# Two cached-attention decodes on one core: q in bank pairs, four products in a row, single heads at the end

## The chip, the cores and the metric

The kernel runs on 1 core of one Trainium2 chip. The metric is the device time of one execution in microseconds (us); the median of several runs is compared. The kernel before takes 674.53 us (median of 3 runs, 673.84 to 674.82).

## The reference

Two independent attention blocks, A and B, each decode one token. All tensors are bf16.

```python
def _A_ref(x, k_cache, v_cache, wq, wo):        # x [1,1,512], caches [1,32,8192,128]
    q = (x @ wq).reshape(B, Sq, 32, 128).transpose(0, 2, 1, 3)
    scores = einsum("bhqd,bhkd->bhqk", q, k_cache) * (128 ** -0.5)
    p = softmax(scores, axis=-1)
    o = einsum("bhqk,bhkd->bhqd", p, v_cache)
    return o.transpose(0, 2, 1, 3).reshape(B, Sq, 4096) @ wo      # wo [4096, 512]
# _B_ref is the same with B's inputs (32 query heads, 32 key heads)
return concatenate([a, b], axis=-1)
```

For each block 32 heads read a K cache and a V cache of 2 MiB a head, and `wq` and `wo` are 4 MiB each. Together that is 272 MiB, 285.2 MB, read once; the arithmetic on it is small.

## The kernel before

The caches are worked through in 16 **quads** of 4 heads (`NM` = 16: quads 0 to 7 of A, 8 to 15 of B). A quad's K is 8 MiB, laid out as 128 partitions of 64 KiB: partition 32h + p holds 256 consecutive keys of head h. Its V has the same layout. `kn` holds two quads of K, `vn` one quad of V. At the start `vn` holds both `wq`; at the end `kn` holds both `wo`.

**Loads.** SyncE (SP) issues every load, in one fixed order, with semaphore waits in between (lines 190 to 210): wq of A, x of A and B, wq of B, K0, K1, V0, K2, V1, then K(n+1) and V(n) in turn, then wo. V0 waits until q has left `vn` (`s_q`), K2 until TensorE has read quad 0's products out of `kn` (`s_red`), V(n) until the matmuls with V(n-1) are done (`s_pv`), and K(n+1) until the first product of quad n (`s_mul`). A load later in the order is not issued before an earlier one, whatever it needs itself. After the last K come all of wo of A, wo of B's first 16 heads, the last V in two pieces (cut at key `VCUT` of each partition's 256), and wo of B's other heads in the pieces of the table `WOB`. `WP` names pieces that are loaded in two parts, partitions 0 to 119 and 120 to 127.

**q.** TensorE begins in the block `pe_first`. x is broadcast into `xb`, then x @ wq is formed in four groups (A and B, two each) of 16 matmuls: 4 PSUM banks of `big`, 4 matmuls a bank (line 353). ScalarE (ACT) copies the 4 banks to `qbc` in bf16 (line 376), 32 partitions of each, and only then TensorE starts the next group (line 358).

**A quad.** VectorE (DVE) multiplies K in place by q, broadcast over the keys, in four products of 64 keys (`mul`, line 427). TensorE sums each product over the 128 dims down to 8 partial sums, with 16 matmuls against the identity that add up in one PSUM bank (a *chunk*, lines 256 and 259). DVE adds these 8 (`sr`, line 432) to get scores. A chunk uses bank c % 2 of `big`, so chunk 2 waits for `sr(0)` and chunk 3 for `sr(1)`. DVE's order is `mul(0) mul(1) mul(2) sr(0) mul(3) sr(1) sr(2) sr(3)`; then it takes the maximum, and ACT does four exponentials into `pt`.

**V.** TensorE's loop (line 247) does quad n's four chunks first and then quad n-1's V matmuls: the sums of the exponentials (line 298), 64 matmuls of `pt` with `vn` (line 309), and, after ACT's copy of the result (line 382), 8 small matmuls that lay the heads out as columns (line 315). The last round has no chunks: it multiplies wo of A and of B's first 16 heads instead (line 281), then does the V matmuls of quad 15. In these, before the second piece of V, it issues 8 matmuls with a zero vector (line 304) and then waits for that piece (`s_v1`).

**The end.** Heads 16 to 31 of B go through `oz`, whose columns are the stationary operands of `rows(g)` (line 231), 4 matmuls a head. Heads 28 and 29 get there by way of `zb`, one matmul and a copy (lines 491, 323 and 494), heads 30 and 31 by a copy (line 492). DVE copies the result (line 496), and SP and ACT store it (line 502).

Of the kernel before, what the change touches and what calls it, by code (L numbers as in the profile page):

```python
# [6 lines left out]
ALU = mybir.AluOpType  # L7
# [7 lines left out]
def bass_concat_heads__mha_block_cached__gqa_block_cached__decode_kernel(  # L15
# [14 lines left out]
    ks = [A_k_cache, B_k_cache]  # L30
# [3 lines left out]
    NA = 2  # L34
# [4 lines left out]
    C = D // P  # L39
# [19 lines left out]

    WOB = [(0, 16), (16, 8), (24, 4), (28, 2), (30, 1), (31, 1)]  # L60
    HT = 16
    RG = [32, 16, 8, 4, 2]
    WP = {2: 120}
    VCUT = T - CT
    NQ = NOUT // P
    QR = P // NQ

    with ExitStack() as st:
# [5 lines left out]
        def flat(ap):  # L74
            return ap.rearrange("p t d -> p (t d)")
# [4 lines left out]
        assert T * Dh == NA * W  # L80
        wq_v = flat(vn[:]).rearrange("p (a c j i h d) -> p a c j i h d", a=NA, c=C, j=2, i=4, h=G)
        KX = 1
# [112 lines left out]
        load_k(1, (s_xm, 2))  # L195
        load_v(0, (s_q, 4 * NA * 2))
        load_k(2, (s_red, RED), (s_k, 32))
# [18 lines left out]
        e = nc.tensor  # L216
        rw, rq = [e.alloc_register("pe_" + x) for x in ("rw", "rq")]
        n1, k1, rv, ko = [e.alloc_register("pe_" + x) for x in ("n1", "k1", "rv", "ko")]
        nc.br("pe_first", engines=[nc.tensor.engine])
        with nc.body("pe_main", valid_engines=[nc.tensor.engine]):  # L220
# [16 lines left out]
            e.reg_mov(k1, 1)  # L237
            e.reg_mov(rv, 0)
            e.reg_mov(ko, 0)
            e.wait_ge(c_pool, POOL)  # L240

# [5 lines left out]
            with e.Fori(0, NM + 1) as n:  # L247
                nr = e.alloc_register("pe_nr")
                e.reg_sub(nr, n1, 1)
                with e.If_lt(nr, NM):  # L250
                    with e.Fori(0, NCH) as c:
                        e.wait_ge(s_mul, k1)
                        e.wait_ge(s_sr, k1)
                        e.reg_add(k1, k1, 1)
                        o = big[:, bass.ds(c % 2, 1), :].rearrange("p o (t d) -> p (o t) d", d=DW)
                        e.matmul(o, ident[:], chunk(0), start=True, stop=False, skip_group_check=True)  # L256
                        with e.Fori(0, RL):
                            for u in range(RU):
                                i = e.matmul(o, ident[:], chunk((1 + u) * DW), start=False,  # L259
                                             stop=(u == RU - 1), skip_group_check=True)  # L260
# [35 lines left out]
                with e.If_ne(nr, 0):  # L296
                    e.wait_ge(s_p, n1)
                    e.matmul(misc[:, 0:G], ones_f[:], rsum[:], start=True, stop=True).then_inc(s_sum, 1)  # L298
                    e.wait_ge(s_v, rv)
                    for j in range(T // NT):  # L300
                        if j * NT == VCUT:
                            with e.If_eq(nr, NM):
                                for _ in range(8):
                                    e.matmul(big[0:1, 0, :], zero[:], wo_sb[:, 0, :], start=True,
                                             stop=True)
                                e.wait_ge(s_v1, 16)
# [11 lines left out]
                e.reg_add(n1, n1, 1)  # L318
                e.reg_add(rv, rv, 16)
# [12 lines left out]
        with nc.body("pe_first", valid_engines=[nc.tensor.engine]):  # L332
            for r, v in ((rw, 1), (rq, G)):
                e.reg_mov(r, v)
            e.sem_inc(s_sum, 1)
            e.sem_inc(s_turn, 1)
            e.sem_inc(s_w[1], 1)
            e.wait_ge(s_x, 16 * NA)
            e.wait_ge(c_on, 1)
            for a in range(NA):  # L340
# [6 lines left out]
            with e.Fori(0, NA) as a:  # L347
                e.wait_ge(s_w[1], rw)
                e.reg_add(rw, rw, 16)
                with e.Fori(0, 2) as j:  # L350
                    with e.Fori(0, G) as hh:
                        for c in range(C):
                            i = e.matmul(  # L353
                                big[:, bass.ds(hh, 1), :].rearrange("p o (i d) -> p (o i) d", d=Dh),
                                xb[:, a, c, :], wq_v[:, a, c, j, :, hh, :],
                                start=(c == 0), stop=(c == C - 1))
# [8 lines left out]
        rq, n1 = [e.alloc_register("act_" + x) for x in ("rq", "n1")]  # L365
        e.reg_mov(rq, G)
        e.reg_mov(n1, 1)
        e.sem_inc(s_p, 1)
        for a in range(NA):
            e.wait_ge(s_xm, a + 1)  # L370
            e.copy(xb[:, a].rearrange("p c m -> p (c m)"), (misc, tps)[a]).then_inc(s_xb, 1)  # L371
        with e.Fori(0, NA * 2) as j:
            e.wait_ge(s_q, rq)
            for hh in range(G):
                q = slice(hh * HP, (hh + 1) * HP)
                e.copy(qbc[q, bass.ds(j * 4, 4), :].rearrange("p i d -> p (i d)"),  # L376
                       big[q, hh, :]).then_inc(s_qc, 1)
            e.reg_add(rq, rq, G)
        e.wait_ge(c_pool, POOL)
# [24 lines left out]
        s_o = sem("s_o")  # L404
        for r, v in ((n1, 1), (k5, RL), (rk, 16), (kt, 0), (ks, NCH + 2)):
            e.reg_mov(r, v)
        e.sem_inc(s_sr, 2)
        e.sem_inc(s_k, 16)
# [8 lines left out]
        i.then_inc(c_sel, 1)  # L417
        e.wait_ge(s_qc, 2 * G)
        e.wait_ge(s_k0, 16)
        with e.Fori(0, NM):  # L420
# [9 lines left out]
            def sr(c):  # L430
                e.wait_ge(s_red, k5)
                e.tensor_reduce(s_sb[:, c * CT:(c + 1) * CT],  # L432
                                big[:, c % 2, :].rearrange("p (t d) -> p t d", d=DW),
                                AX.X, ALU.add).then_inc(s_sr, 1)
# [98 lines left out]
```

## Time and profile before

| what | value |
|---|---|
| median of 3 runs | 674.53 us |
| the profiled execution, its own time | 674.37 us |
| its span, first to last instruction | 673.1 us |
| busy: PE, DVE, ACT | 405.5, 337.0, 80.9 us |
| moved by DMA | 285.24 MB, mean 424 GB/s |
| DMA engines busy, share of the span | 98.5% |

The profile divides the span into 40 slices of 16.8 us; a row gives each slice's DMA rate. Windows give the same for any stretch: a DMA packet counts where it starts, with all its bytes, so in a short window a packet of 64 KiB can be counted by itself. The PE clock in the profile is the share of full speed that TensorE was granted. "Released by" names what ended a wait; "issue" is time in which the profile shows nothing waited for. Times below are from the span's start unless a duration is meant.

### The profile page before, as it was taken

How to read it: one execution, taken by the hardware profiler on the slowest of the kernel's cores; microseconds unless marked ns; L12 is line 12 of the kernel's file. 1: busy time of each engine (PE TensorE's matmuls, PEld its weight loads, DVE VectorE, ACT ScalarE, POOL GpSimd, SP SyncE). 2: the span in 40 equal slices, each digit the busy share in tenths (PEclk: the TensorE clock that was granted, in tenths of full speed). 3: DMA queues.
4: the chain of work that ended last, by engine and by line, in shares of the span. 5: the costliest groups of instructions: out<-in, count | busy, mean ns of one | idle time of the engine just before them, and what ended most of it. 6: DMA issues, size and time to landing. Idle time of an engine off the chain costs nothing.

```text
span 673.1 us, 8068 instructions
## 1 busy us (share of the span) xinstructions
PE 405.5 (60%) x2415; PEld 168.2 (25%) x2415; DVE 337.0 (50%) x218; ACT 80.9 (12%) x182; POOL 2.4 (0%) x13
## 2 busy tenths in 40 slices
PE   1667595919376481927558192855729194663986
PEld 0222232303122130313223031322313031221333
DVE  1036676638092654719174471908356280926510
ACT  1211202020202002020200202020110202020020
POOL 1000000000000000000000000000000000000000
PEclk9767897969779596977869596886959687795987
DMA  9999987999999999999999999999999999999898
GB/s 373 438 436 436 432 378 312 436 436 436 436 436 436 436 436 432 421 417 425 425 436 436 436 436 436 436 436 436 436 436 436 436 436 436 436 436 436 387 439 297
DMA packets 6071, 285.24 MB, mean 424 GB/s; under 512 B 690, under 2 KB 949, under 8 KB 1205
## 3 DMA queue, kind: packets, MB, share of 16 engines
q1 hardware_dynamic: 6063, 285.22, 98.5%
q8 instruction: 1, 0.02, 0.0%
q14 instruction: 1, 0.01, 0.0%
q10 hardware_dynamic: 6, 0.00, 0.0%
HBM read 285.21 MB, written 0.00 MB: 424 GB/s over the span
## 4 chain that ended last, share of the span: by engine, by line
DMA 72%; DVE 11%; PE 10%; issue 4%; ACT 1%; SPq 1%; DVEq 0%; ACTq 0%
DMA kn<-in_B_k_cache_dram 40%; DMA kn<-in_A_k_cache_dram 25%; DVE kn L427 10%; PE big L259 5%; DMA kn<-in_B_wo_dram 4%; PE big L353 4%; DMA kn<-in_B_x_dram 2%; ACT qbc L376 1%; PE acc L309 1%; DVE s_sb L432 1%; SPq L173 1%; PE big L256 0%; DVEq L422 0%; PE tps L315 0%; ACT acc_sb L371 0%
## 5 line engine op out<-in xcount | busy, mean ns | idle before, releaser
L427 DVE TENSOR_TENSOR kn<-kn,qbc x64 | 280.1, 4419 | 155.6 <-DMA kn<-in_B_k_cache_dram 70.7
L259 PE MATMUL big<-kn,ident 128*128 x960 | 266.3, 419 | 0.0
L256 PE MATMUL big<-kn,ident 128*128 x64 | 28.1, 440 | 216.5 <-DVE kn L427 196.4
L259 PEld LDWEIGHTS big<-kn,ident 128*128 128x128 bf16 x960 | 100.8, 105 | 149.7 <-issue 99.4
L432 DVE TENSOR_REDUCE s_sb<-big 128x64 f32<-128x512 f32 x64 | 42.7, 686 | 73.4 <-PE big L259 73.4
L382 ACT COPY acc_sb<-acc 128x512 f32<-128x512 f32 x16 | 9.4, 585 | 474.9 <-PE acc L309 474.8
L256 PEld LDWEIGHTS big<-kn,ident 128*128 128x128 bf16 x64 | 6.3, 98 | 234.8 <-issue 232.9
L309 PE MATMUL acc<-vn,pt 128*16 128x512 bf16 x1024 | 60.5, 387 | 2.4 <-DMA vn<-in_B_v_cache_dram 2.4
L388 ACT ACTIVATE pt<-s_sb,negb 32x256 bf16<-32x256 f32 x64 | 54.8, 857 | 1.3
L452 DVE TENSOR_TENSOR oD<-tps,rinv 128x4 f32 x16 | 2.6, 162 | 75.8 <-PE tps L315 75.7
L353 PE MATMUL big<-vn,acc_sb 128*128 x64 | 25.2, 579 | 12.9 <-issue 12.9
L309 PEld LDWEIGHTS acc<-vn,pt 128*16 128x16 bf16 x1024 | 24.7, 91 | 29.9 <-DMA vn<-in_B_v_cache_dram 2.5
L315 PE MATMUL tps<-tsel,acc_sb 128*128 128x4 f32 x128 | 16.9, 255 | 11.1 <-ACT acc_sb L382 10.4
L315 PEld LDWEIGHTS tps<-tsel,acc_sb 128*128 128x128 f32 x128 | 15.5, 191 | 19.1 <-ACT acc_sb L382 17.9
L353 PEld LDWEIGHTS big<-vn,acc_sb 128*128 x64 | 8.7, 135 | 29.3 <-issue 28.0
L388 ACT ACTIVATION_READ_ACCUMULATOR pt<-s_sb,negb 32x1 f32 x64 | 15.9, 248 | 0.0
L376 ACT CAST qbc<-big 32x512 f32 x16 | 9.2, 576 | 30.8 <-PE big L353 30.5
L281 PE MATMUL big<-kn,o 128*1 x48 | 12.2, 418 | 0.0
L298 PE MATMUL misc<-rsum,ones_f 128*128 128x4 f32 x32 | 6.0, 259 | 6.9 <-issue 6.2
L384 ACT ACTIVATE negb<-gm 128x1 f32<-128x1 f32 x16 | 3.2, 203 | 46.3 <-DVE gm L455 46.3
L342 PE MATMUL misc<-ones_bf,kn 1*128 1x128 bf16 x4 | 0.6, 302 | 13.2 <-DMA kn<-in_B_x_dram 13.2
L298 PEld LDWEIGHTS misc<-rsum,ones_f 128*128 128x128 f32 x32 | 4.8, 188 | 13.8 <-issue 13.8
(50 smaller groups left out, 40.9 us busy)
## 6 DMA issues: line engine op xcount, KB each, us to landing
vn<-in_B_v_cache_dram SPq DMA_DIRECT2D x1, 6144.0 KB, 20.5
vn<-in_A_wq_dram SPq DMA_DIRECT2D x1, 4096.0 KB, 13.7
vn<-in_B_wq_dram SPq DMA_DIRECT2D x1, 4096.0 KB, 22.3
kn<-in_A_wo_dram SPq DMA_DIRECT2D x1, 4096.0 KB, 24.3
kn<-in_B_wo_dram SPq DMA_DIRECT2D x1, 2048.0 KB, 28.9
vn<-in_B_v_cache_dram SPq DMA_DIRECT2D x1, 2048.0 KB, 25.1
kn<-in_B_wo_dram SPq DMA_DIRECT2D x1, 1024.0 KB, 27.4
kn<-in_B_wo_dram SPq DMA_DIRECT2D x1, 480.0 KB
```

Of the source, the lines that this page charges most:

```text
L256: e.matmul(o, ident[:], chunk(0), start=True, stop=False, skip_group_check=True)
L259: i = e.matmul(o, ident[:], chunk((1 + u) * DW), start=False, stop=(u == RU - 1), skip_group_check=True)
L281: i = e.matmul(y, o2[:, bass.ds(h + u, 1)], wo_sb[:, h + u, :], start=False, stop=False, skip_group_check=True)
L298: e.matmul(misc[:, 0:G], ones_f[:], rsum[:], start=True, stop=True).then_inc(s_sum, 1)
L309: i = e.matmul(acc[q:q + NT * G, :], pt[:, ts, :].rearrange("p t g -> p (t g)"), vn[:, ts, :].rearrange("p t d -> p (t d)"), start=(j < NP ...
L315: i = e.matmul(tps[:, 0:G], acc_sb[:, t * Dh:(t + 1) * Dh], tsel[:, t * G:(t + 1) * G], start=(t == 0), stop=(t == NT - 1))
L353: i = e.matmul(big[:, bass.ds(hh, 1), :].rearrange("p o (i d) -> p (o i) d", d=Dh), xb[:, a, c, :], wq_v[:, a, c, j, :, hh, :], start=(c = ...
L376: e.copy(qbc[q, bass.ds(j * 4, 4), :].rearrange("p i d -> p (i d)"), big[q, hh, :]).then_inc(s_qc, 1)
L382: e.copy(acc_sb[:], acc).then_inc(s_acc, 1)
L388: i = e.activation(pt[q, :, h], s_sb[q, :], AF.Exp, bias=negb[q, :], scale=scale, accum_out=rsum[q, h:h + 1])
L427: e.tensor_tensor(k, k, qbc[:, bass.ds(n, 1), :].broadcast_to([P, CT, Dh]), ALU.mult).then_inc(s_mul, 1)
L432: e.tensor_reduce(s_sb[:, c * CT:(c + 1) * CT], big[:, c % 2, :].rearrange("p (t d) -> p t d", d=DW), AX.X, ALU.add).then_inc(s_sr, 1)
```

## The change

Line numbers of the changed kernel differ by a few; the names are the same.

- **q in pairs.** A pair of banks (8 matmuls) has one semaphore count, and ACT waits for a pair, not for four banks. TensorE no longer waits behind a group of 16 but ahead of each pair, on a count of ACT's copies (`s_qc`, 2 a copy, and 7 to begin with). The one register `rq`, raised by 3 a pair and by 4 more at each of A and B, serves this wait and that for wq. V0's load waits for 8 pairs (`NA * 4`) where it waited for 16 banks.
- **Four products in a row.** `mul(0..3)` then `sr(0..3)`; chunk c uses bank c of `big`.
- **The end.** `VCUT` moves from key 192 to 224, so the last V comes in 7 MiB and 1 MiB (before: 6 and 2). The zero matmuls are 4, not 8. Wo of B's heads 28 to 31 comes in four loads of one head (before: two heads, one, one). The tables for groups of two are gone, and the last four heads go from the V matmuls to `oz` in one DVE operation.
- **One DMA engine spared.** `WP` names piece 3 (head 28, 1 KiB a partition) beside piece 2 (heads 24 to 27, 4 KiB a partition): 5 KiB a row for partitions 120 to 127.

```diff
-    WOB = [(0, 16), (16, 8), (24, 4), (28, 2), (30, 1), (31, 1)]
+    WOB = [(0, 16), (16, 8), (24, 4), (28, 1), (29, 1), (30, 1), (31, 1)]
-    RG = [32, 16, 8, 4, 2]
-    WP = {2: 120}
-    VCUT = T - CT
+    RG = [32, 16, 8, 4]
+    WP = {2: 120, 3: 120}
+    QC = 7
+    VCUT = T - 32
...
-        load_v(0, (s_q, 4 * NA * 2))
+        load_v(0, (s_q, NA * 4))
...
-                        o = big[:, bass.ds(c % 2, 1), :].rearrange("p o (t d) -> p (o t) d", d=DW)
+                        o = big[:, bass.ds(c, 1), :].rearrange("p o (t d) -> p (o t) d", d=DW)
...
-                                for _ in range(8):
+                                for _ in range(4):
...
             got_wo(e, 1)
             rows(1)
-            e.wait_ge(t_dve, 9)
-            tp.of(relayout(zps, 0, 2))
             got_wo(e, 2)
             rows(2)
-            e.wait_ge(t_dve, 11)
+            e.wait_ge(t_dve, 9)
             for g in range(3, len(WOB)):
...
             with e.Fori(0, NA) as a:
-                e.wait_ge(s_w[1], rw)
-                e.reg_add(rw, rw, 16)
+                e.wait_ge(s_w[1], rq)
+                e.reg_add(rq, rq, 4)
                 with e.Fori(0, 2) as j:
-                    with e.Fori(0, G) as hh:
-                        for c in range(C):
-                            i = e.matmul(
-                                big[:, bass.ds(hh, 1), :].rearrange("p o (i d) -> p (o i) d", d=Dh),
-                                xb[:, a, c, :], wq_v[:, a, c, j, :, hh, :],
-                                start=(c == 0), stop=(c == C - 1))
+                    with e.Fori(0, 2) as u:
+                        e.wait_ge(s_qc, rq)
+                        e.reg_add(rq, rq, 3)
+                        for v in range(2):
+                            for c in range(C):
+                                i = e.matmul(
+                                    big[:].rearrange("p (u v) (i d) -> p u v i d", v=2, d=Dh)[
+                                        :, bass.ds(u, 1), v].rearrange("p o i d -> p (o i) d"),
+                                    xb[:, a, c, :], wq_v[:, a, c, j, :, u, v, :],
+                                    start=(c == 0), stop=(c == C - 1))
                         i.then_inc(s_q, 1)
-                    e.wait_ge(s_qc, rq)
-                    e.reg_add(rq, rq, G)
...
         with e.Fori(0, NA * 2) as j:
-            e.wait_ge(s_q, rq)
             for hh in range(G):
+                if hh % 2 == 0:
+                    e.wait_ge(s_q, rq)
+                    e.reg_add(rq, rq, 1)
                 q = slice(hh * HP, (hh + 1) * HP)
                 e.copy(qbc[q, bass.ds(j * 4, 4), :].rearrange("p i d -> p (i d)"),
-                       big[q, hh, :]).then_inc(s_qc, 1)
-            e.reg_add(rq, rq, G)
+                       big[q, hh, :]).then_inc(s_qc, 2)
...
-            mul(0)
-            mul(1)
-            mul(2)
+            for c in range(NCH):
+                mul(c)
             e.wait_ge(s_p, n1)
-            sr(0)
-            mul(3)
-            sr(1)
-            sr(2)
-            sr(3)
+            for c in range(NCH):
+                sr(c)
...
-        e.tensor_tensor(oD[:, NA * H - G:], tps[:, 0:G], rinv[:], ALU.mult).then_inc(s_o, 1)
-        e.wait_ge(s_o, NM + 1)
-        spread(1, 28, 2, 0)
-        td.of(e.tensor_copy(oz[:, 14:16, QR - 1], oD[:, NA * H - 2:]))
+        td.of(e.tensor_tensor(oz[:, HT - G:, QR - 1], tps[:, 0:G], rinv[:], ALU.mult))
         e.wait_ge(t_pe, 5)
-        td.of(e.tensor_copy(oz[:, 12:14, QR - 1], zps[:, 0:2]))
-        e.wait_ge(t_pe, 6)
```

DVE's loop over the quads, before (L427 is `mul`, L432 `sr`, the waits in brackets are semaphores):

```order
L427 TENSOR_TENSOR kn<-kn,qbc 128x8192
L427 ISA
L427 TENSOR_TENSOR kn<-kn,qbc 128x8192
L432 TENSOR_REDUCE s_sb<-big 128x64 [waits s_red,s_p]
L435 ISA
L427 TENSOR_TENSOR kn<-kn,qbc 128x8192
L432 TENSOR_REDUCE s_sb<-big 128x64 [waits s_red]
L435 REGISTER_ALU
```

and with the change:

```order
L427 TENSOR_TENSOR kn<-kn,qbc 128x8192
L427 ISA
L427 TENSOR_TENSOR kn<-kn,qbc 128x8192
L427 ISA
L427 TENSOR_TENSOR kn<-kn,qbc 128x8192
L432 TENSOR_REDUCE s_sb<-big 128x64 [waits s_red,s_p]
L435 REGISTER_ALU
L432 TENSOR_REDUCE s_sb<-big 128x64 [waits s_red]
```

The last product now stands ahead of `sr(0)` and of its waits for TensorE (`s_red`) and for the previous quad's exponentials (`s_p`).

SP's last loads, before (`kn` takes wo, `vn` the last V; partitions x elements):

```order
L173 DMA vn<-in_B_v_cache_dram 128x24576 [waits s_pv]
L173 DMA vn<-in_B_v_cache_dram 128x8192
L173 DMA kn<-in_B_wo_dram 128x4096
L173 DMA kn<-in_B_wo_dram 120x2048
L173 DMA kn<-in_B_wo_dram 8x2048
L173 DMA kn<-in_B_wo_dram 128x1024
L173 DMA kn<-in_B_wo_dram 128x512 x2
```

and with the change:

```order
L174 DMA vn<-in_B_v_cache_dram 128x28672 [waits s_pv]
L174 DMA vn<-in_B_v_cache_dram 128x4096
L174 DMA kn<-in_B_wo_dram 128x4096
L174 DMA kn<-in_B_wo_dram 120x2048
L174 DMA kn<-in_B_wo_dram 8x2048
L174 DMA kn<-in_B_wo_dram 120x512
L174 DMA kn<-in_B_wo_dram 8x512
L174 DMA kn<-in_B_wo_dram 128x512 x3
```

SP issues two loads more after the last V; the bytes and the wait ahead of them are the same.

More of the change, by code (lines that the diff above doesn't have):

```diff
@@ L216, in bass_concat_heads__mha_block_cached__gqa_block_cached__decode_kernel @@
         e = nc.tensor
-        rw, rq = [e.alloc_register("pe_" + x) for x in ("rw", "rq")]
+        rq = e.alloc_register("pe_rq")
         n1, k1, rv, ko = [e.alloc_register("pe_" + x) for x in ("n1", "k1", "rv", "ko")]
@@ L332, in bass_concat_heads__mha_block_cached__gqa_block_cached__decode_kernel @@
         with nc.body("pe_first", valid_engines=[nc.tensor.engine]):
[L333 to L337, printed above, removed]
+            e.reg_mov(rq, 1)
+            for c in (s_sum, s_turn, s_w[1]):
+                e.sem_inc(c, 1)
             e.wait_ge(s_x, 16 * NA)
-            e.wait_ge(c_on, 1)
+            e.wait_ge(c_pool, POOL)
             for a in range(NA):
@@ L404, in bass_concat_heads__mha_block_cached__gqa_block_cached__decode_kernel @@
         s_o = sem("s_o")
-        for r, v in ((n1, 1), (k5, RL), (rk, 16), (kt, 0), (ks, NCH + 2)):
+        for r, v in ((n1, 1), (k5, RL), (rk, 16), (kt, 0), (ks, 2 * NCH)):
             e.reg_mov(r, v)
-        e.sem_inc(s_sr, 2)
+        e.sem_inc(s_sr, NCH)
         e.sem_inc(s_k, 16)
@@ L432, in sr @@
                 e.tensor_reduce(s_sb[:, c * CT:(c + 1) * CT],
[L433 removed]
+                                big[:, c, :].rearrange("p (t d) -> p t d", d=DW),
                                 AX.X, ALU.add).then_inc(s_sr, 1)
                 e.reg_add(k5, k5, RL)
[L437 to L439 removed]
+            for c in range(NCH):
+                mul(c)
             e.wait_ge(s_p, n1)
[L441 to L445 removed]
+            for c in range(NCH):
+                sr(c)
             e.wait_ge(s_sr, ks)
```

12 lines of the change are left out of this document (6 added, 6 removed).

## The prediction

> **What bounds the kernel now.** The page first: the DMA rate by slice and the chain of waits.
>
> ```profile
> GB/s 373 438 436 436 432 378 312 436 436 436 436 436 436 436 436 432 421 417 425 425 436 436 436 436 436 436 436 436 436 436 436 436 436 436 436 436 436 387 439 297
> DMA 72%; DVE 11%; PE 10%; issue 4%; ACT 1%; SPq 1%; DVEq 0%; ACTq 0%
> ```
>
> The load stream is the bound: 285.2 MB at the plateau of 436 GB/s is 654 us of the 673.1 us span. A faster engine gives nothing where the rate is 436. What can be won is a hole in the stream. There is one, in slices 5 and 6: (436 - 378 + 436 - 312) / 436 x 16.8 us is 7.0 us of lost transfer. SP's loads and windows on both sides show it.
>
> ```profile
> 52.37 0.33 SPq L173 DMA_DIRECT2D vn<-in_A_v_cache_dram  x1
> 75.40 0.33 SPq L173 DMA_DIRECT2D kn<-in_A_k_cache_dram  x1
> 105.23 0.33 SPq L173 DMA_DIRECT2D vn<-in_A_v_cache_dram  x1
> ...
> 96.70:97.70 1.00, 1.00 (x4) 0.36 (x5) 0.12 (x1) 0.00 (x0) 0.00 (x0) 1.00 2.27 983
> 98.70:98.85 0.15, 0.15 (x2) 0.11 (x2) 0.00 (x0) 0.00 (x0) 0.00 (x0) 1.00 1.02 437
> 99.50:106.10 6.60, 5.53 (x74) 2.40 (x73) 1.20 (x3) 0.58 (x1) 0.00 (x0) 1.00 0.00 0
> 106.10:106.65 0.55, 0.55 (x7) 0.55 (x7) 0.00 (x0) 0.00 (x0) 0.00 (x0) 1.00 5.41 1787
> 143.20:143.70 0.50, 0.00 (x0) 0.00 (x0) 0.00 (x0) 0.00 (x0) 0.00 (x0) 0.50 3.63 1573
> ```
>
> K2 ends, nothing starts from 99.5 to 106.1, and V1, issued at 105.23, restarts the stream. The last number of a window row is GB/s; times its length, over 65,536 bytes, it counts packets: 15 started at 96.7 to 97.7 (K2's last on 15 engines), **one more at 98.7**, 15 at 106.1, and 12 at 143.2 to 143.7 (K3's last ones; none follows). So one of the 16 DMA engines is a straggler, 1.0 to 2.0 us behind the others (I take 1.7) until the hole, where it catches up because the others stand idle.
>
> V1 waits for quad 0's V matmuls, and TensorE does those after quad 1's chunks.
>
> ```profile
> 15.95 6.08 PE L353 MATMUL big<-vn,acc_sb 128*128 x16 [1.74 <-issue]
> 22.16 2.38 ACT L376 CAST qbc<-big 32x512 f32 x4 [7.28 <-PE big L353]
> 25.60 6.37 PE L353 MATMUL big<-vn,acc_sb 128*128 x16 [3.57 <-issue]
> 45.86 6.48 PE L353 MATMUL big<-vn,acc_sb 128*128 x16 [3.54 <-issue]
> 52.48 2.38 ACT L376 CAST qbc<-big 32x512 f32 x4 [7.64 <-PE big L353]
> ...
> 44.01 13.10 DVE L427 TENSOR_TENSOR kn<-kn,qbc  x3 [39.79 <-ACT qbc L376]
> 56.91 0.60 PE L256 MATMUL big<-kn,ident 128*128 x1 [4.57 <-issue]
> 62.83 0.38 PE L256 MATMUL big<-kn,ident 128*128 x1
> 66.46 0.39 PE L256 MATMUL big<-kn,ident 128*128 x1
> 63.71 4.42 DVE L427 TENSOR_TENSOR kn<-kn,qbc  x1
> 71.22 0.39 PE L256 MATMUL big<-kn,ident 128*128 x1 [0.62 <-issue]
> 75.41 0.69 DVE L432 TENSOR_REDUCE s_sb<-big 128x64 f32<-128x512 f32 x1 [4.08 <-PE big L259]
> 77.58 13.10 DVE L427 TENSOR_TENSOR kn<-kn,qbc  x3 [0.50 <-issue]
> ...
> 82.37 0.61 PE big L256
> 96.68 0.39 PE big L256
> 101.62 3.59 PE acc L309 x64
> 112.38 33.97 DMA kn<-in_A_k_cache_dram
> 151.07 33.95 DMA kn<-in_A_k_cache_dram
> ```
>
> q's matmuls and copies take turns: 16.0 to 54.9, about 10 us a group. DVE has quad 0's first product at 48.4, but TensorE starts its chunk at 56.9, after q. From there all is late: quad 0 is summed at 75.4, quad 1 starts at 77.6, V0's matmuls end at 105.2. Later quads have slack: K3 lands at 146.35, K4 at 185.02, 38.67 us a quad, all of it transfer.
>
> **The change, part by part.**
>
> *q in pairs.* Eight pairs of 8 matmuls. If TensorE stayed at the slow pace of these rows (6.48/16 is 0.405 us) a pair takes 3.3 us. The next pair of the same banks needs two copies (2 x 0.6 us), and those run under the other pair. By the counts, the second pair of A, and of B, also waits for the first copy of the pair just made: 0.7 us and a restart of 1.1 us (22.16 + 2.38 to 25.60), and B's first pair for 7 copies, about the same and 0.5 for the loop. That is 15.95 + 8 x 3.3 + 3 x 1.9, so 48 us, and 49.5 with the last copies. At 0.216 us a matmul (the zero matmuls quoted below, 1.08 us for five steps) it is about 37. Either way earlier than 54.86; I take 40 to 48. V0's issue moves forward too, at no gain: wq, K0 and K1 fill the queue to 60.
>
> *Quad 0.* Its first product ends at 44.01 + 4.42, as before, since DVE waits there for K0 (the row names ACT's copies, but the eight needed were long made). TensorE starts 0.37 us later (77.58 + 4.42 to 82.37), at 48.8. Chunks by the rows above: 5.9 us, then 3.6, 3.6, and 4.2 for the last with its end: 66.1 instead of 75.4. (The fourth product is ready at 44.01 + 13.10 + 4.35, so 61.5, just before chunk 3 can start.) Then 2.17 us to the next quad, as from 75.41 to 77.58: **quad 1 starts at 68.3**, 9.3 us earlier. K1 is there: wq, K0 and K1, 25.2 MB at 433 GB/s from the start, and the straggler's lag make about 62.
>
> *Four products in a row.* In quad 1 chunk 3 started 19.1 us after the first product (96.68 - 77.58), behind `sr(0)`, `mul(3)` and `sr(1)`. Now it needs four products, 17.45 us, and 0.36 to start: 17.8, so 1.3 us less. The `sr` that moved run under chunk 3. What queues behind the moved wait for the exponentials is only `sr`, no product. From chunk 3 to the end of the V matmuls it took 105.21 - 96.68 = 8.5 us. So V1 is issued at 68.3 + 17.8 + 8.5 = **94.6, not 105.23**. A load's first packets come 0.9 to 1.4 us after its issue (105.23 and 106.10 to 106.65), and the engines run dry from 99.1 on (96.7 + 2.4 a packet). It is 3.5 us early: the hole closes whole. In later quads the 1.3 us only add to the slack.
>
> *What the hole is worth.* For 15 engines: K3's last packets start at 143.45 instead of 97.2 + 38.67 = 135.9, so 7.6 us. For the straggler: 143.5 - (98.78 + 38.67) = **6.05 us**. Without the hole the straggler stays 1.7 us behind to the end, and every load counts as landed only when its share has. So from K3 on all moves forward by 6.05.
>
> *The end.* Rows of the tail:
>
> ```profile
> 639.74 2.60 SPq L173 DMA_DIRECT2D kn<-in_B_wo_dram  x6
> 671.74 0.27 SPq L502 DMA_DIRECT2D out_dram<-out_q  x1
> ...
> 659.47 4.33 PE L309 MATMUL acc<-vn,pt 128*16 128x512 bf16 x48 [2.43 <-DMA vn<-in_B_v_cache_dram]
> 663.63 1.46 PE L304 MATMUL big<-kn,zero 128*1 128x512 bf16 x6
> 666.44 0.58 ACT L399 COPY acc_sb<-acc 128x512 f32<-128x512 f32 x1 [11.06 <-PE acc L309]
> 667.08 1.06 PE L315 MATMUL tps<-tsel,acc_sb 128*128 128x4 f32 x8 [0.70 <-ACT acc_sb L399]
> 668.07 0.63 PE L231 MATMUL yrow<-kn,oz 128*32 128x128 bf16 x32
> 671.07 0.29 PE L231 MATMUL yrow<-kn,oz 128*32 128x128 bf16 x4 [0.18 <-DMA kn<-in_B_wo_dram]
> ...
> 659.40:662.60 3.20, 3.13 (x32) 1.16 (x36) 0.00 (x0) 0.00 (x0) 0.00 (x0) 0.50 1.01 430
> 662.70:663.70 1.00, 1.00 (x21) 0.45 (x14) 0.00 (x0) 0.00 (x0) 0.00 (x0) 1.00 0.86 360
> 60.00:65.00 5.00, 5.00 (x21) 1.97 (x20) 1.90 (x2) 0.00 (x0) 0.00 (x0) 0.81 1.00 433
> ```
>
> Before, the last wo is the limit: TensorE's final four matmuls wait for it until 671.07, and 2.03 us later the span ends. With the change the first piece of V is 1 MiB larger, 2.4 us at 433 GB/s, so on the old clock TensorE starts at 661.9. It is then at half clock (PEclk 0.50) for 3.2 us as here, or 5.0 as at quad 0 (start 56.9; 0.81 over 60 to 65 puts the rise at 61.9); I take 3.8. At 4.33/48 = 0.09 us that is 42 matmuls; 14 more at 0.056 (3.59/64), four zero matmuls at 0.216, eight more and the last one's latency: 3.8 + 0.8 + 0.9 + 0.5 + 0.3 = 6.3 us. ACT's copy comes at 668.2 (before 666.44: half of the zero matmuls saved, but begun later). Then as before 1.63 us to `rows`, 0.63 + 0.3 + 0.3 us of them (the relayout and two DVE steps are gone), and the final four start at 671.0 less latency. Shifted by 6.05, at **664.95**. Wo's own landing moves from 671.07 by 7.6 to 663.5 on 15 engines; on the straggler to 665.0, less the 40 KiB (1.5 us) it is spared if it is the spared engine. So TensorE's chain or a tie sets the end: 664.95 + 2.03 is a span of 667.0. The two added loads cost their issue (0.43 us each, 2.60/6, some 25 us ahead of need) and small-packet time on the 15 engines that have 1.5 us to spare.
>
> The profiled time was 674.37 for a span of 673.1; 667.0 + 1.27 is 668.3. The median shown is 674.53, so **668.4 us**. Bounds of the tail: half clock for 3.2 us, -0.2; for 5.0, +0.4. A lag of 1.0 or of 2.0 us instead of 1.7 gives 667.7 or 668.7.
>
> A rule speaks for a longer tail. By the Trainium skill (TensorE: Matmul & The Clock Gate, "The HAM clock gate"), the clock rises after a busy window of about 3.4 us that runs freely, so the wait could be anything up to two windows. At 6.8 us all 56 matmuls and the zero ones would be slow, and the sum 669.6; these traces show 3.2 to 5.0.
>
> **The rivals.** (a) *The straggler sets nothing*: the 7.6 us come whole, because the lag is not carried on. V and wo land 7.6 earlier, the final four start at 663.5, time **666.9**. For: TensorE's chain then ends at 663.4, a tie. Against: the one packet at 98.7, still there after three loads.
>
> (b) *Part of the gain stays out.* The straggler too stands idle once V1 is issued after 99.2 (105.23 - 6.05), that is, if TensorE starts quad 0 after 53.4. Started at 56.9 as before, 3.5 of the 6.05 us are gone: **671.9**. Or the two added loads each pay a round of their own: a tiny store pays about 1.3 us from issue to the end (671.74 to 673.1); twice that puts wo at 666.1 instead of 664.95 and the time at **669.5**. Against: eight loads are queued at once, and wo's last ones only wait in line. The Trainium skill (DMA: Bandwidth & Descriptors, "Anatomy of one DMA") has a fixed cost of about 2 us a load, mostly completion; by that, in series, it would be 670.9.
>
> (c) *Slower: the pairs take turns.* If each pair waits for its own copies, as the two counts named above do, q costs 8 x (3.3 + 0.3 + 1.3 + 1.0), and ends at 63; TensorE starts quad 0 at 65 (2.05 us after q, 54.86 to 56.91) and ends it at 82.5, 7.1 after the old, less 1.3 from the four products. Time **680**. It decides once q ends 1.3 us later than 54.86. Against: only two of eight pairs have such a count.
>
> (d) *The hole stays*, because what holds V1 is not q but something not on this chain; only the four products' 1.3 us come, or nothing: **673.2 to 674.5**. For: the chain of waits follows transfers through most of the span. Against: each row from 54.9 to 105.2 releases the next.
>
> **How the numbers follow.** Forecast 0.62; (a) 0.12; (b) 0.13; (c) 0.05; (d) 0.08. The predicted time is the first: 668.4, by itself 667.7 to 669.6. The range reaches down to (a) and into (b), 666.6 to 671.0, leaving out (c), (d) and the far end of (b). A measurement of this kernel tells 0.2%, 1.35 us, from no change. Faster: forecast, (a), (b), and a little of (d), 0.88. The same: most of (d), 0.07. Slower: (c), 0.05.
>
> **What would show it.** Right: no window near 99 without DMA, slices 5 and 6 at 436; V1 issued near 95; chunk 0 of quad 0 at 49; the same lone late packet still at the end of each load; at the tail the first piece's matmuls x56 start near 655.8 and the final four wait for no DMA, or barely. Wrong: a hole left at 99 (b, d); q's pairs 5 us apart (c); loads landing together after 100 (a); a final wait for wo beyond 665 (b).

## The result, and the profile after

| kernel | median, us | runs | lowest to highest |
|---|---|---|---|
| before | 674.63 | 6 | 673.84 to 675.35 |
| changed | 668.30 | 6 | 667.98 to 669.23 |

The ratio is 0.9909, with an interval of 0.9897 to 0.9922: 6.3 us less. The profiled execution took 668.23 us with a span of 667.0, the span that the prediction had summed up. In the third set of experiments below the same two kernels are only 4.6 us apart (668.41 and 672.99, ratio 0.9924, 0.9911 to 0.9938): the changed kernel comes out the same, the kernel before is faster there.

The page of the changed kernel: its span, the DMA rate in 40 slices of 16.7 us, and the chain of waits.

```profile
span 667.0 us, 8062 instructions
GB/s 376 442 436 440 440 440 421 413 428 440 440 436 440 440 436 436 428 413 428 440 440 436 440 436 436 432 417 421 440 440 436 440 440 432 440 424 405 431 454 247
DMA 81%; DVE 11%; issue 4%; PE 3%; DVEq 0%; SPq 0%; ACT 0%
```

Slices 5 and 6 had 378 and 312. They are now at 440 and 421: the hole is closed. (Dips of that size recur along the span, and are there before as well, 417 and 421.) TensorE's share of the chain fell from 10% to 3%.

Its timeline from the first pairs of q to V1 (start, duration, engine, line; idle time and its releaser in brackets):

```profile
15.89 3.23 PE L352 MATMUL big<-vn,acc_sb 128*128 x8 [1.84 <-issue]
20.34 1.89 PE L352 MATMUL big<-vn,acc_sb 128*128 x8 [1.22 <-ACT qbc L377]
...
37.22 1.18 ACT L377 CAST qbc<-big 32x512 f32 x2 [0.76 <-PE big L352]
...
48.63 0.59 PE L256 MATMUL big<-kn,ident 128*128 x1 [11.54 <-DVE kn L427]
...
67.08 0.69 DVE L432 TENSOR_REDUCE s_sb<-big 128x64 f32<-128x512 f32 x1 [3.98 <-PE big L259]
69.24 17.43 DVE L427 TENSOR_TENSOR kn<-kn,qbc  x4 [0.51 <-issue]
74.00 0.58 PE L256 MATMUL big<-kn,ident 128*128 x1 [6.97 <-DVE kn L427]
78.75 0.38 PE L256 MATMUL big<-kn,ident 128*128 x1
83.50 0.38 PE L256 MATMUL big<-kn,ident 128*128 x1 [0.59 <-issue]
88.24 0.38 PE L256 MATMUL big<-kn,ident 128*128 x1 [0.59 <-DVE s_sb L432]
...
96.79 0.33 SPq L174 DMA_DIRECT2D vn<-in_A_v_cache_dram  x1
```

q is done at 38.4 (before 54.86). TensorE now waits 11.54 us for quad 0's first product and begins the chunk the moment it is there, at 48.63 (before 56.91). V1 is issued at 96.79 (before 105.23).

Windows of the changed kernel (last number GB/s; a load's packets are 64 KiB, those of the last V's first piece 56 KiB):

```profile
99.40:99.95 0.55, 0.00 (x0) 0.00 (x0) 0.00 (x0) 0.55 (x2) 0.00 (x0) 1.00 4.32 1787
101.00:101.20 0.20, 0.00 (x0) 0.00 (x0) 0.00 (x0) 0.19 (x1) 0.00 (x0) 0.50 0.76 328
...
636.40:637.50 1.10, 1.10 (x5) 0.26 (x4) 0.00 (x0) 1.08 (x4) 0.00 (x0) 0.52 1.95 842
637.50:638.50 1.00, 1.00 (x4) 0.38 (x3) 0.00 (x0) 0.90 (x4) 0.00 (x0) 0.50 0.13 57
```

Where the kernel before has no packet from 99.5 to 106.1, V1 now follows K2 at once: 15 packets at 99.4 to 99.95 (1787 x 0.55 / 65.5), one at 101.1. The late engine, the prediction's straggler, stays late. 540 us further on, at the last V, 15 packets of 56 KiB start at 636.4 to 637.4 (842 x 1.1 is 926 KB, with four of 16 KiB), and the lone last one after 637.5, at 638.10 by its packet's record in the trace. In the kernel before, all 16 engines start the last V together (983 GB/s x 0.8 us is 16 packets of 48 KiB), as a window of it shows:

```profile
643.90:644.70 0.80, 0.80 (x4) 0.21 (x2) 0.00 (x0) 0.79 (x4) 0.00 (x0) 0.50 2.28 983
```

The end of the changed kernel, timeline:

```profile
655.58 5.52 PE L310 MATMUL acc<-vn,pt 128*16 128x512 bf16 x56 [4.99 <-DMA vn<-in_B_v_cache_dram]
...
662.46 0.58 ACT L399 COPY acc_sb<-acc 128x512 f32<-128x512 f32 x1 [13.52 <-PE acc L310]
664.09 1.20 PE L232 MATMUL yrow<-kn,oz 128*32 128x128 bf16 x64
```

and windows (the number before the last two is the granted clock):

```profile
655.60:660.30 4.70, 4.70 (x48) 1.59 (x52) 0.00 (x0) 0.00 (x0) 0.00 (x0) 0.50 1.01 347
660.40:662.40 2.00, 2.00 (x28) 0.63 (x16) 0.00 (x0) 0.00 (x0) 0.00 (x0) 1.00 0.99 221
662.75:664.60 1.85, 1.50 (x47) 1.49 (x51) 0.17 (x1) 0.30 (x1) 0.00 (x0) 1.00 0.19 53
```

The 64 matmuls of `rows` run without a wait for wo, but only just: the last window still holds 53 GB/s, 98 KB of wo, and the last packet's record is at 664.56. TensorE ran at half clock (0.50) for 4.8 us.

### The profile page after: what moved, and what is told of

It is laid out like the page before. It is cut to its first block, busy times and chain, and to the rows that moved or that the text cites. A ratio compares the mean times of both kernels' runs of the same rounds, so it can differ in the third digit from the quotient of the medians.

```text
span 667.0 us, 8062 instructions
## 1 busy us (share of the span) xinstructions
PE 395.0 (59%) x2410; PEld 164.5 (25%) x2410; DVE 335.8 (50%) x213; ACT 80.9 (12%) x182; POOL 2.4 (0%) x13
## 4 chain that ended last, share of the span: by engine, by line
DMA 81%; DVE 11%; issue 4%; PE 3%; DVEq 0%; SPq 0%; ACT 0%
DMA kn<-in_B_k_cache_dram 41%; DMA kn<-in_A_k_cache_dram 37%; DVE kn L427 11%; DMA vn<-in_B_v_cache_dram 3%; PE acc L310 1%; PE big L259 1%; DVE s_sb L432 0%; DVEq L422 0%; SPq L174 0%; PE yrow L232 0%; DVEq L427 0%; PE tps L316 0%; PE big L256 0%; PE big L305 0%; ACT acc_sb L399 0%
## 5 line engine op out<-in xcount | busy, mean ns | idle before, releaser
L427 DVE TENSOR_TENSOR kn<-kn,qbc x64 | 278.9, 4420 | 159.4 <-DMA kn<-in_A_k_cache_dram 87.5
L432 DVE TENSOR_REDUCE s_sb<-big 128x64 f32<-128x512 f32 x64 | 41.1, 683 | 64.1 <-PE big L259 64.1
L352 PE MATMUL big<-vn,acc_sb 128*128 x64 | 16.4, 403 | 6.6 <-ACT qbc L377 3.6
L352 PEld LDWEIGHTS big<-vn,acc_sb 128*128 x64 | 6.5, 102 | 16.3 <-issue 11.5
```

The source lines that it names most:

```text
L352: i = e.matmul(big[:].rearrange("p (u v) (i d) -> p u v i d", v=2, d=Dh)[:, bass.ds(u, 1), v].rearrange("p o i d -> p (o i) d"), xb[:, a, ...
L427: e.tensor_tensor(k, k, qbc[:, bass.ds(n, 1), :].broadcast_to([P, CT, Dh]), ALU.mult).then_inc(s_mul, 1)
L432: e.tensor_reduce(s_sb[:, c * CT:(c + 1) * CT], big[:, c, :].rearrange("p (t d) -> p t d", d=DW), AX.X, ALU.add).then_inc(s_sr, 1)
```

## The experiments

Three sets of four kernels; each set ran on one chip, together with the kernel before, whose median there was 673.77, 673.36 and 672.99 us. Ratios are to the kernel before of the same set.

### Which part brings the time

**All but the pairs**: the changed kernel with q in four groups of 16 matmuls.

```diff
-                    with e.Fori(0, 2) as u:
-                        e.wait_ge(s_qc, rq)
-                        e.reg_add(rq, rq, 3)
-                        for v in range(2):
+                    with e.Fori(0, G) as hh:
...
+                    e.wait_ge(s_qc, rq)
+                    e.reg_add(rq, rq, G)
```

> The full change but q's matmuls and copies in groups of four banks, as before. If q alone closes the hole: V1 issued at 105.0 or 105.1, the hole of 6.6 us stands, the straggler is gone after it, 674.5 us (674.2 to 674.9). If the four products in a row bring V1 forward by the 1.3 us of the prediction: issue at 103.9, 673.2 us.

Measured: 674.38 us, ratio 1.0003 (0.9988 to 1.0017). SP's timeline:

```profile
105.56 0.33 SPq L174 DMA_DIRECT2D vn<-in_A_v_cache_dram  x1
```

The page's rate by slice:

```profile
GB/s 373 438 436 436 436 374 311 436 436 432 436 436 436 432 432 428 424 424 428 428 432 436 436 436 436 436 436 436 436 436 436 436 436 436 436 432 436 395 434 296
```

The hole stands (374 and 311), and four products in a row, single heads and the spared engine bring nothing by themselves.

**The pairs alone**: the kernel before with q in pairs, nothing else.

```diff
-                    with e.Fori(0, G) as hh:
+                    with e.Fori(0, 2) as u:
+                        e.wait_ge(s_qc, rq)
+                        e.reg_add(rq, rq, 3)
+                        for v in range(2):
...
-                    e.wait_ge(s_qc, rq)
-                    e.reg_add(rq, rq, G)
```

> The kernel before with q in pairs alone (old product order, old last loads, old spare). If the hole in the load stream is all of the gain and q alone closes it: V1 issued near 97, no stretch without DMA near 100, everything after it 6.05 us earlier, 668.3 us (668.0 to 669.0), as the full change. If the tail's edits carry part of the gain: 669.5 to 671. If the one spare of the old kernel already hits the straggler: 666.9.

Measured: 669.19 us, ratio 0.9926 (0.9913 to 0.9939). Its timeline:

```profile
97.71 0.33 SPq L174 DMA_DIRECT2D vn<-in_A_v_cache_dram  x1
...
665.27 0.40 PE L232 MATMUL yrow<-kn,oz 128*32 128x128 bf16 x16 [0.40 <-DMA kn<-in_B_wo_dram]
666.08 0.84 PE L232 MATMUL yrow<-kn,oz 128*32 128x128 bf16 x16 [0.40 <-DMA kn<-in_B_wo_dram]
```

V1 is issued 7.5 us earlier, and 4.6 us of the gain are there, out of 5.5 in this set. The rest of the change is worth 0.9 us on top (669.19 against 668.27 and 668.24 for two kernels of this set, below, that differ from the changed one in little); alone it was worth nothing. The end of this kernel still waits twice for wo. (Its program also had a second 16 KiB transfer of instructions, at 27 us, and three late engines, so part of the 0.9 may be due to that.)

### What the hole is worth, and to whom

The prediction holds that 15 engines have 1.4 to 1.7 us to spare, since everything lands with the late one. Then V1 may be issued later at no cost, until the late engine too stands idle. Two kernels delay V1 alone. The first waits until quad 0's heads are laid out:

```diff
-        load_v(1, (s_pv, 2))
+        load_v(1, (s_pv, 2), (s_turn, 2))
```

> The change, with V1 issued one step later: after quad 0's heads are laid out (about 98.5 us) instead of after its V matmuls (96.79). Theory A, the prediction's margin: 15 engines idle for 0.5 to 1.7 us near 99.5, but the late one is busy with K2 until 101.1 and loses nothing; the loads land as its share does, so the time is 668.2 to 668.8, the same. Rival B: at 96.8 there is no slack left, since a load needs 2 to 3 us from issue to its first packet on the last engine while the stream runs, and each further microsecond counts whole: 1.7 us more, 669.8 to 670.2.

Measured: 668.54 us (667.97 to 670.56), ratio 0.9932 (0.9916 to 0.9947); the changed kernel in this set: 668.41. SP's timeline:

```profile
98.61 0.33 SPq L174 DMA_DIRECT2D vn<-in_A_v_cache_dram  x1
```

Windows at V1 and at the last V:

```profile
99.10:99.50 0.40, 0.00 (x0) 0.00 (x0) 0.00 (x0) 0.37 (x2) 0.00 (x0) 1.00 0.02 0
99.50:99.95 0.45, 0.00 (x0) 0.00 (x0) 0.00 (x0) 0.45 (x2) 0.00 (x0) 0.62 6.20 2039
...
636.40:637.90 1.50, 1.50 (x5) 0.49 (x4) 0.00 (x0) 1.47 (x5) 0.00 (x0) 0.50 1.79 770
637.90:638.50 0.60, 0.60 (x3) 0.15 (x2) 0.00 (x0) 0.53 (x2) 0.00 (x0) 0.50 0.22 96
```

V1 is 1.82 us later. Engines run dry (no packet starts from 99.1 to 99.5), and V1's first packets start 1.0 to 1.6 us after the issue. At the last V the 15 start at 637.15 to 637.69, some 0.7 us later than in the changed kernel; the late one's lone packet (96 x 0.6 is one of 56 KiB) starts at 638.11, where it was 638.10. **The late engine lost nothing, and so the kernel lost nothing.**

The second waits for quad 1's exponentials:

```diff
-        load_v(1, (s_pv, 2))
+        load_v(1, (s_pv, 2), (s_p, 3))
```

> The change, with V1 issued after quad 1's exponentials, at about 102.75 us, 5.96 later. Theory A: 15 engines stand idle from 99.6 to about 104, but what counts is the late engine, dry at 101.13 and started again by about 103.8 to 104: 2.5 to 3.0 us lost, and the lag of 1.4 us gone: 670.8 to 671.9. Rival B, every microsecond of issue counts: 5.96 more, 674.0 to 674.3, as slow as before although V1 is still issued 2.5 us earlier than there.

Measured: 672.07 us, ratio 0.9981 (0.9971 to 0.9991), 3.66 us above the changed kernel of the set. SP's timeline:

```profile
103.13 0.33 SPq L174 DMA_DIRECT2D vn<-in_A_v_cache_dram  x1
```

Windows of this kernel:

```profile
101.40:103.10 1.70, 0.00 (x0) 0.00 (x0) 1.04 (x1) 1.64 (x4) 0.00 (x0) 0.68 0.00 0
...
642.10:642.70 0.60, 0.60 (x2) 0.13 (x1) 0.00 (x0) 0.58 (x1) 0.00 (x0) 0.50 3.55 1529
```

V1 is 6.34 us later than in the changed kernel, the time 3.66: the delay counts from an issue at about 103.13 - 3.66 = 99.5. After the idle stretch all 16 engines start the last V together (1529 x 0.6 is 16 packets of 56 KiB). The time is 0.2 us above the range I gave, since V1 came 0.4 us later than I had read from the profile. The rival, by which each microsecond of issue counts, is out by 2 us here and by 1.5 in the run before.

### Four products in a row

The changed kernel with the old order of DVE and the banks c % 2:

```diff
-            for c in range(NCH):
-                mul(c)
+            mul(0)
+            mul(1)
+            mul(2)
             e.wait_ge(s_p, n1)
-            for c in range(NCH):
-                sr(c)
+            sr(0)
+            mul(3)
+            sr(1)
+            sr(2)
+            sr(3)
```

> The change with the old order of DVE (mul 0, 1, 2, sr 0, mul 3, sr 1, 2, 3) and banks c % 2. Theory now: TensorE's own pitch of 4.75 us a chunk, not the order of the products, sets the last chunk. Then in quad 1 chunk 3 starts 19.0 to 19.2 us after the first product as in the change (19.0), V1 is issued at 96.7 to 97.1, and the time is 668.2 to 668.5, the same. Rival, the prediction's step: four products in a row are worth 1.3 us there. Then chunk 3 starts 20.3 us after the first product, V1 is issued at 98.0 to 98.2, still before the engines run dry at 99.5, and the time is 668.3 to 668.9.

Measured: 669.33 us (667.67 to 669.91), ratio 0.9935 (0.9914 to 0.9955). Its timeline of quad 1:

```profile
69.41 13.10 DVE L427 TENSOR_TENSOR kn<-kn,qbc  x3 [0.51 <-issue]
...
88.54 0.39 PE L256 MATMUL big<-kn,ident 128*128 x1 [0.66 <-DVE s_sb L432]
...
97.09 0.33 SPq L174 DMA_DIRECT2D vn<-in_A_v_cache_dram  x1
```

Chunk 3 starts 19.13 us after the first product; with the change it is 88.24 - 69.24 = 19.00. The order is worth 0.1 us there and 0.3 us at V1's issue, not 1.3. The timeline of the kernel before shows why: its chunk 3 has two chains ahead of it.

```profile
95.53 1.29 DVE L432 TENSOR_REDUCE s_sb<-big 128x64 f32<-128x512 f32 x2
...
92.17 3.92 PE L259 MATMUL big<-kn,ident 128*128 x15
96.68 0.39 PE L256 MATMUL big<-kn,ident 128*128 x1 [0.58 <-DVE s_sb L432]
```

DVE's chain ends with `sr(1)`, at about 96.2 (95.53 and 0.69 for the first of the two). TensorE's own ends with chunk 2, at 92.17 + 3.92 = 96.09. The new order takes DVE's chain away, and TensorE's stays where it was.

The time is above the 668.2 to 668.5 that I expected, by more than 0.3 us of issue can explain while there is slack. In its profile V1's last share landed 20.1 us after K2's, where the changed kernel took 19.3. Why is not shown, and since no unaltered kernel ran in this set, I don't put the 0.9 us down to the order.

### The end: two limits

**No engine spared**:

```diff
-    WP = {2: 120, 3: 120}
+    WP = {}
```

> The full change with no wo load split in 120 and 8 partitions: two loads fewer, 40 KiB (1.5 us) more for the engine that was spared. If the straggler is another engine, the spared one has that time to give: 668.3 us as it is, at most 0.2 less. If the spared engine is the straggler: wo lands 1.5 us later, 669.8 us.

Measured: 668.27 us, ratio 0.9908 (0.9894 to 0.9922). A window of its end:

```profile
662.75:664.60 1.85, 1.15 (x21) 1.10 (x24) 0.00 (x0) 0.58 (x1) 0.00 (x0) 1.00 0.00 0
```

Its timeline there:

```profile
664.47 1.07 PE L232 MATMUL yrow<-kn,oz 128*32 128x128 bf16 x64
```

After 662.75 no packet of wo starts: its last record is at 662.70, 1.9 us earlier than with the sparing, and the time is the same. Sparing an engine does not bring wo in earlier; whole pieces do. But TensorE's chain sets the end here (`rows` starts at 664.47 and waits for nothing), so nothing is gained by it alone.

**The old cut**: key 192 and 8 zero matmuls, in the changed kernel.

```diff
-    VCUT = T - 32
+    VCUT = T - CT
...
-                                for _ in range(4):
+                                for _ in range(8):
```

> The change with the last V cut at key 192 (6 and 2 MiB) and 8 zero matmuls, as before. In the change's own profile wo's last packet is at 664.56 and the final matmuls wait for nothing, so TensorE's chain and wo are within a microsecond. Theory A: wo's landing on the spared engine's fellows and the straggler is a tie with TensorE; TensorE's first piece starts 2.4 us earlier, ACT's copy comes 1.8 us earlier, but the final four matmuls then wait for wo until about 664.5 to 665.0: 668.0 to 668.5, the same. Theory B: TensorE's chain alone sets the end: 666.5 to 667.0.

Measured: 668.76 us (668.23 to 669.33), ratio 0.9931 (0.9912 to 0.995). Its timeline:

```profile
661.47 0.59 ACT L399 COPY acc_sb<-acc 128x512 f32<-128x512 f32 x1 [12.34 <-PE acc L310]
...
664.17 1.57 PE L232 MATMUL yrow<-kn,oz 128*32 128x128 bf16 x32 [0.45 <-DMA kn<-in_B_wo_dram]
```

TensorE's copy comes 1.0 us earlier, and `rows` now waits for wo: the gain turns into a wait. (This program also had a second 16 KiB transfer of instructions, at 27 us, and V1 at 97.63, so half a microsecond of its wo may be due to that.)

**Both at once**: no engine spared and the old cut, in two sets, the second time beside the unaltered changed kernel.

```diff
-    WP = {2: 120, 3: 120}
-    VCUT = T - 32
+    WP = {}
+    VCUT = T - CT
...
-                                for _ in range(4):
+                                for _ in range(8):
```

> No engine spared and the old cut (key 192, 8 zero matmuls). Without the sparing alone wo's last packet was at 662.70 instead of 664.56 and TensorE set the end at the same 667.2. If both ends are limits side by side, then taking 1.8 us off TensorE's chain (copy at 660.6 instead of 662.5) and 1.9 us off wo gives a span of 665.2 to 665.8 and 666.4 to 667.0 us. Rival: wo's last packet comes at 662.70 but its completion counts about 1.5 us later, as a load's does elsewhere, so the final four wait for it: 667.3 to 668.0. Second rival: nothing moves, 668.3, if TensorE's slow clock takes back what the earlier start gives.

> No engine spared and the last V cut at key 192 with 8 zero matmuls, once more, now beside the unaltered change on the same chip: 666.3 to 666.9, 1.6 to 2.0 us under it. If the two ends are not both limits and the earlier gain came from the set of runs, the difference is under 0.5 us.

> The change once more, unaltered, beside the three others of this set: 668.2 to 668.5 by every theory. It gives the spread between sets of runs, and the clock against which the two delays and the shorter end are read.

Measured: 666.44 us (666.34 to 666.89), ratio 0.9896 (0.9878 to 0.9915); then 666.49 (666.36 to 667.1), ratio 0.9896 (0.988 to 0.9912), beside 668.41 (668.15 to 668.55) for the changed kernel. **1.9 us less, from two edits of which neither gave anything alone**, and under both kernels of this study. Timeline of the second:

```profile
653.71 5.11 PE L310 MATMUL acc<-vn,pt 128*16 128x512 bf16 x48 [2.87 <-DMA vn<-in_B_v_cache_dram]
...
661.46 0.58 ACT L399 COPY acc_sb<-acc 128x512 f32<-128x512 f32 x1 [12.28 <-PE acc L310]
663.09 1.07 PE L232 MATMUL yrow<-kn,oz 128*32 128x128 bf16 x64
```

The unaltered kernel of that set shows the tie from its other side, in its timeline:

```profile
655.54 4.73 PE L310 MATMUL acc<-vn,pt 128*16 128x512 bf16 x56 [3.72 <-DMA vn<-in_B_v_cache_dram]
...
663.25 2.28 PE L232 MATMUL yrow<-kn,oz 128*32 128x128 bf16 x64
```

and in a window:

```profile
658.50:659.00 0.50, 0.50 (x12) 0.23 (x8) 0.00 (x0) 0.00 (x0) 0.00 (x0) 0.81 1.34 393
```

Here the clock rose after 3.15 us of work (0.81 over 658.5 to 659.0 puts it at 658.69), TensorE was at `rows` 0.84 us earlier than in the first profile, and `rows` took 2.28 us instead of 1.20: it waited inside for wo's last pieces, whose last packet's record is at 664.79. The span is 667.2 against 667.0. What TensorE's clock gives, wo takes back. (`rows` went on with the last head at 665.29, 0.5 us after that packet; no run shows the 1.5 us that I had put between a load's last packet and its count.)

### What makes one engine late

In the profile of each kernel so far one transfer of instructions, 16 KiB on a queue of its own, begins at 2 to 3 us, when the first wq does. I put the late engine down to it. In the next kernel TensorE's first block stands in line, ahead of the main one; in the changed kernel it is reached by a jump and left by another:

```diff
-        nc.br("pe_first", engines=[nc.tensor.engine])
+        e.reg_mov(rq, 1)
+        for c in (s_sum, s_turn, s_w[1]):
+            e.sem_inc(c, 1)
...
+        nc.br("pe_main", engines=[nc.tensor.engine])
...
-        with nc.body("pe_first", valid_engines=[nc.tensor.engine]):
-            e.reg_mov(rq, 1)
-            for c in (s_sum, s_turn, s_w[1]):
-                e.sem_inc(c, 1)
...
-            nc.br("pe_main", engines=[nc.tensor.engine])
```

> The full change with TensorE's first block (x and q) placed ahead of its main block instead of behind it, so that TensorE does not jump at the start. If the 16 KiB instruction transfer at 2 us is that jump's and makes the straggler: no such transfer at the start, K2's last packets all within 1 us, everything lands up to 1.5 us earlier, 666.9 us. If the transfer has another cause: it stays at 2 us, the straggler too, 668.3 us.

Measured: 668.24 us, ratio 0.9913 (0.99 to 0.9926). Windows of this kernel, K0 to K1 and K2 to V1:

```profile
58.00:58.70 0.70, 0.70 (x4) 0.26 (x3) 0.70 (x1) 0.00 (x0) 0.00 (x0) 1.00 3.46 1498
...
99.00:99.80 0.80, 0.00 (x0) 0.00 (x0) 0.00 (x0) 0.78 (x3) 0.00 (x0) 1.00 2.85 1229
100.75:100.95 0.20, 0.00 (x0) 0.00 (x0) 0.00 (x0) 0.20 (x1) 0.00 (x0) 0.50 0.76 328
```

and windows of the changed kernel:

```profile
58.10:58.70 0.60, 0.56 (x3) 0.32 (x4) 0.60 (x1) 0.00 (x0) 0.00 (x0) 1.00 3.78 1638
59.85:59.95 0.10, 0.10 (x2) 0.03 (x1) 0.10 (x1) 0.00 (x0) 0.00 (x0) 1.00 1.51 655
```

Near 58, all 16 engines start together (1498 x 0.7 is 16 packets), where the changed kernel has 15 and one 1.3 to 1.8 us later. The instruction transfer is now at 70.29 and takes 1.05 us. The packets' records show what it does: 15 engines start a packet at 70.11 to 70.73, the sixteenth only at 71.32, as the transfer ends, and its packet takes 2.92 us in place of 2.42. From there on one engine is late again: 15 packets near 99.4, one at 100.84. So the lag comes with that transfer, wherever it falls. Its size fits too: in the eight profiles with this one transfer, at 2 us, it takes 1.14 to 2.06 us, and the late engine starts its last packet of K2 0.95 to 1.93 us behind the mean of the others, each time 0.1 to 0.3 us less than the transfer took. By the Trainium skill (Runtime: NRT & Kernel Launch, "Instruction fetch mechanics") instructions come in blocks of 16 KiB over a DMA queue, and a taken branch out of the loaded pages forces such a fetch. The traces agree in the size and in the queue of its own; of the branch they show that without the jump no transfer falls at 2 us. The lag here is 1.4 us, and the time is unchanged: the transfer moved, as one theory had it, but the lag came back with it.

**Inline, whole pieces, old cut** together: the two edits of the end in the inline kernel.

```diff
-    WP = {2: 120, 3: 120}
-    VCUT = T - 32
+    WP = {}
+    VCUT = T - CT
...
-                                for _ in range(4):
+                                for _ in range(8):
```

> The same as whole_cut, with TensorE's first block written inline, which moves the 16 KiB instruction transfer from 2 us to about 70 us and leaves a lag of 1.1 instead of 1.4 us on one engine. Theory: the end follows the straggler, so 0.3 us less than whole_cut, 666.1 to 666.7. Rival: the straggler's lag no longer counts once wo is in whole pieces, and both are equal.

Measured: 666.29 us (666.13 to 666.65), ratio 0.9895 (0.9874 to 0.9915), the fastest kernel here, though not to be told from the 666.44 beside it.

## Why the prediction was right, and where it was not

- **The hole comes from q's turns, and the pairs close it.** Right: with the pairs alone V1 is issued at 97.71, without them at 105.56. q ends at 38.4, under the 40 to 48 that I took. A pair of 8 matmuls after the first takes 1.89 us, 0.236 each, so TensorE was near its full pace (my other end, 37), not the slow pace that I chose. It made no difference, since quad 0 waits for its product until 48.63 (predicted 48.8).
- **Four products in a row save 1.3 us.** Wrong, and it is the step that failed. I took the last chunk to be held by DVE's order alone. With the change the four starts, 74.00, 78.75, 83.50 and 88.24, are 4.75 us apart: a chunk's 16 matmuls take 4.15 and the gap to the next 0.59. DVE makes a product every 17.43 / 4 = 4.36 us, so TensorE is the slower one. In the kernel before it was done with chunk 2 only 0.1 us ahead of `sr(1)`, and so taking `sr(1)` away could not give more than that. Quad 0 has the same error: I took 3.6 us for its third chunk, though my own rows have 4.76 (66.46 to 71.22, with no wait but issue). It took 4.74, quad 0 was summed at 67.08, not 66.1, and quad 1 began 0.9 us later than predicted.
- **V1 at 94.6, 3.5 us early.** It came at 96.79. The later start of quad 1 and the missing 1.3 us cost 2.2 us of the margin. The hole closed all the same, since the margin of 3.5 us was larger than the error. The margin itself was sized about right: 98.61 costs nothing, and 103.13 costs as if it began at 99.5 (predicted: 99.2, when the late engine runs dry).
- **The hole is worth 7.6 us to 15 engines, 6.05 to the late one, and the late one counts.** Right. At the last V the late engine moved from at most 644.4 to 638.10, some 6.3 us, and the others from about 644.2 to 636.7, 7.5 us. The delayed kernels show both halves: a delay that only the 15 feel costs nothing, and one that the late engine feels removes its lag. The lag in the changed kernel was 1.6 us at K2 and 1.4 at the last V, not 1.7, within the 1.0 to 2.0 that I had bounded. Rival (a), that the lag is not carried on, falls with the lone packet at 638.10.
- **The tail.** TensorE began at 655.58 (655.8 predicted), its copy came at 662.46 (662.1), `rows` ended at 664.09 + 1.20 = 665.29, which puts the start of the final four, 0.29 earlier, at 665.0 (664.95); the span ended at 667.0. That the sum comes out to 0.05 us is luck: TensorE began 0.3 us early, took 6.9 us to the copy instead of 6.3, and then 2.5 us to the final four instead of 2.8. Half clock lasted 4.8 us here, not 3.8; over the runs it lasted from 3.15 us (the second profile) to 5.5 (no engine spared), wider than the 3.2 to 5.0 that I had. The tie that I named decides: with TensorE 0.84 us faster, as in the second profile, the time does not fall. The spared engine was not the late one: in the changed kernel's packet rows the late engine loads its share of the split pieces.
- **The two added loads.** I priced them at their issue and at some time for small packets that 15 engines had to spare. A wait of their own, part of rival (b), does not show in the time. But the split pieces cost wo 1.9 us, which TensorE hides: its last packet is at 664.56 with them and at 662.70 with whole ones. It is the splitting, not the number of loads. The 128 packets of 4 KiB (heads 24 to 27) take 0.27 us each in the changed kernel, 0.26 in the kernel before, where this piece is split too, and 0.16 where it is whole; yet the kernel before has no more wo loads behind the last V than the kernel with whole pieces, six. The 512 packets of 1 KiB take 0.069 us split and 0.047 whole. Over 16 engines this makes 1.5 of the 1.9 us. Why the packets take longer is open.

Rivals (c) and (d) are out: no pair waits for copies except at the three places that the prediction names, with gaps of 1.2 us, and the rate at 99 is full.

## What to carry to other kernels

Before you credit a reordering, work out every chain that leads to the start you want to move, the consumer's own among them. Here DVE's ended at 96.2 and TensorE's at 96.1: removing one gains no more than the distance to the other. A consumer with the longer period (4.75 us a chunk here, against 4.36 a product) is a sign of it. In a saturated load stream, follow the latest DMA engine, not the mean: slack of the others is free, and an early issue beyond it buys nothing. Where two chains end together, an edit of either shows no gain; test them as a pair before you drop one.

## What was not expected

- One 16 KiB transfer of instructions makes one DMA engine 1 to 2 us late, and in the changed kernel the lag is still there 635 us later; it went only where the engines stood idle (the hole, and the later of the two delays). A jump in TensorE's program decided when it falls (2 or 70 us). Programs with q in pairs and 8 zero matmuls instead of 4 had two such transfers, the second at 27 us, and more than one engine late; in the inline form the second fell at 664.7.
- In some executions more engines fall behind during V1. Nine of its 16 shares land 0.8 us or more after the first with no engine spared, five with the old order of products, four and two in the unaltered kernel's second and first profile, one with V1 at 98.61, though V1's issue lies between 96.6 and 98.6 in all of them. The cause is open.
- The kernel before ran between 670.41 and 675.82 us over the three sets, and between 672.05 and 674.92 without the pairs. The changed kernel ran between 667.98 and 669.23 us in its first set and 668.15 and 668.55 in the last, but it had fewer runs. Whether the hole makes a kernel spread more, and why the kernel before was 0.9 to 1.6 us faster in the three sets than at first, is open.
